# Decoding kept out of the products of sums, and the first two pieces' sums emitted early, in a fused attention and MLP kernel on one core

## The chip, the core and the metric

The kernel runs on one core of one Trainium2 chip. The time is device microseconds of one execution; three executions of the kernel before are given by their median. The engines are TensorE (PE; its weight loads PEld overlap with its matmuls), VectorE (DVE), ScalarE (ACT), GpSimd (POOL) and SyncE (SP), which issues the loads. Each engine takes its instructions in the order in which the program emits them, and an instruction that waits holds up all that stand behind it on its engine.

## The reference

Three stages follow each other. Only the second is touched by the change.

```python
x = banded_attention(q, k, v)              # [2, 768, 512]
h = x.transpose(0, 2, 1) @ U @ V           # mixing along the sequence
u = x + h.transpose(0, 2, 1)
x2 = u + np.maximum(u @ w_ch1, 0) @ w_ch2  # w_ch1 [512, 2048], w_ch2 [2048, 512]
out = gated_mlp(x2, w_in, w_spatial, b_spatial, w_out)
```

The weights come as 64-bit floats and have to be made into 32-bit ones on the chip.

## The kernel before

**Weights.** `Weights` cuts the weights into 28 pieces of 128x1024 elements. Quarter g (0 to 3) of the 2048 hidden columns owns pieces 4g and 4g+1 (columns of `w_ch1`) and 4g+2 and 4g+3 (rows of `w_ch2`). `emit32` decodes a piece in two halves of 128x512: a load by SP into one of three buffers r, a magnitude on ACT (L78, w<-r), and on DVE L83, L84 (w<-w), L90 and L93 (w<-r,w). `emit` then splits a decoded piece w into a high part on ACT (L217, h<-w) and a low part on POOL (L59, l<-w,h), two subtractions of 128x512. There are two buffers for w: piece p can begin only when POOL has read piece p-2 for the last time.

**Sums.** For the first two pieces of quarters 1 to 3 (`quartered`), `quarters` replaces the four blocks of w by differences, in place, with four subtractions on DVE (L234), and splits them as well: th on ACT (L236), tl on POOL (L59). So w comes free only behind tl. For chunks 0 and 1 of 512 tokens, `chunks_by_sums` then makes the products with seven block products instead of eight, fourteen groups of six matmuls for a quarter. The order is X0, X1, Y0, Y1 with h and l, then a pair with S2 (into X), a pair with S1 (into Z), a pair "uh, th" that the text calls S3 (into X), a pair with S4 (into Z) and a last pair. ACT copies (L345, p<-mmm) hold partial results: one of X0 and one of X1 before the S2 pair may write to X, and one of each S2 result before S3 may. A sum is evicted by DVE (L349, s<-mmm,p), ACT (L470, c<-s) and DVE (L471, c<-s,c). The sums S of the activations are made once, in quarter 0, by `sum_rows`: four subtractions on DVE (L325), four copies on ACT (L327) and four subtractions on POOL, twice.

**Order of the work.** A quarter goes: c0, c1 (hidden activations of chunks 0 and 1; by sums in quarters 1 to 3), y0, c2, y1, y2 (outputs of the chunks), where c2 and each y have four groups of twelve matmuls. Groups write to eight PSUM banks in turn, so that a group needs the bank of the group eight before it: y1's that of y0's. DVE frees it, by L471 behind a c group (after L470 on ACT) and L528 (u<-u,mmm) behind a y group. The text writes y1(2) for the group d=2 of y1.

**What emits the decoding.** `run` yields after each group, and `fast` then calls `wt.step(DECODE[1])`, which lets `emit` go on and gives 1.5 us of credit to `emit32`. The rest of the order is plain: what is emitted first stands first on its engine.

Of the kernel before, what the change touches and what calls it, by code (L numbers as in the profile page):

```python
# [52 lines left out]
START, DECODE, MIXING = 20, (0.9, 1.5), (1, 4)  # L53
# [4 lines left out]
def sub(eng, out, a, hi):  # L58
    eng.tensor_tensor(out=out, in0=a, in1=hi.bitcast(F32), op=ALU.subtract)  # L59


def sub_parts(eng, out, a, hi, n):

    m = a.shape[1] // n
    for i in range(n):
        part = slice(i * m, (i + 1) * m)
        sub(eng, out[:, part], a[:, part], hi[:, part])
# [51 lines left out]
class Weights:  # L119
# [88 lines left out]
    def emit(self):  # L208

        nc = self.nc  # L210
        for p, (_, _, a, n) in enumerate(self.order):
            while p >= self.decoded or p - RING >= self.freed:
                yield
            hi = self.ring.tile([P, a, n], F32R, name=f"h{p}", tag="whi")
            lo = self.ring.tile([P, a, n], F32R, name=f"l{p}", tag="wlo")
            wv = self.w32.pop(p)[:, :a * n].rearrange("p (a n) -> p a n", a=a)
            nc.scalar.activation(out=hi, in_=wv, func=AF.Copy)  # L217
            sub_parts(nc.gpsimd, lo, wv, hi, 2)
            if p in self.quartered:
                yield  # L220
                while self.room is None or p - 3 > self.freed:
                    yield
                self.sums[p] = self.quarters(wv)
            self.ready.append((hi, lo))
            yield
# [35 lines left out]
class Moe:  # L261
# [199 lines left out]
    def run(self, u, late):  # L461
# [7 lines left out]
        def evict_c(cp, cc, f):  # L469
            nc.scalar.activation(out=cc[:, 0, f], in_=cp, func=AF.Relu)  # L470
            nc.vector.scalar_tensor_tensor(out=cc[:, 1, f], in0=cp, scalar=0.0, in1=cc[:, 0, f].bitcast(F32),  # L471
                                           op0=ALU.max, op1=ALU.subtract)
# [3 lines left out]
        for g in range(4):  # L476
            w1 = w.take(2)
            w2 = None
            for what, ch in (("c", 0), ("c", 1), ("y", 0), ("c", 2), ("y", 1), ("y", 2)):
                tok = slice(ch * CH, (ch + 1) * CH)  # L480
                if what == "c":
                    cs[ch] = self.q.tile([P, 2, 4, CH], F32R, name="c", tag="Q")
                    if self.room and g and ch < 2:
                        if ch == 1:
                            sums = [w.sums.pop(4 * g + i) for i in range(2)]
                            for _ in self.chunks_by_sums(u, w1, sums, bank, evict_c, cs):
                                yield "g"
                        continue

                    def term(f, ds):  # L490
                        wh, wl = w1[f // 2]
                        fs = slice((f % 2) * P, (f % 2 + 1) * P)
                        return [(wh[:, d, fs], wl[:, d, fs], uh[:, d, tok], ul[:, d, tok]) for d in ds]

                    late_d = g == 0 and ch == 1
                    cps = []
                    if late_d:
                        for f in range(4):
                            cps.append(bank())
                            self.gemm(cps[f], term(f, range(ND - 1)), last=False)  # L500
                            yield "g"
                    for f in range(4):
                        if late_d:
                            cp = cps[f]
                            self.gemm(cp, term(f, [ND - 1]), first=False)
                        else:
                            cp = bank()
                            self.gemm(cp, term(f, range(ND)))
                        evict_c(cp, cs[ch], f)
                        if ch == NCH - 1 and f % 2:  # L510
                            w.free(1)
                        yield "g"
                    if self.room and ch == 1:
                        self.sum_rows(u, 0)
                    continue
                if w2 is None:
                    w2 = w.take(2)
                if g == 3 and ch == 1:
                    x2 = self.pair("x2")
                cc = cs.pop(ch)  # L520
                for d in range(ND):
                    yp = bank()
                    ds = slice(d * P, (d + 1) * P)
                    self.gemm(yp, [(w2[f // 2][0][:, f % 2, ds], w2[f // 2][1][:, f % 2, ds], cc[:, 0, f], cc[:, 1, f])
                                   for f in range(4)])
                    if self.room and g == ch == 0 and d == 1:
                        self.sum_rows(u, 1)
                    nc.vector.tensor_tensor(out=u32[:, d, tok], in0=u32[:, d, tok], in1=yp, op=ALU.add)  # L528
                    if g == 3 and ch:

                        for k in ((), (0, 1), (2,))[ch]:
                            tk = slice(k * CH, (k + 1) * CH)
                            nc.scalar.activation(out=x2[0][:, d, tk], in_=u32[:, d, tk], func=AF.Copy)
                            sub(nc.gpsimd, x2[1][:, d, tk], u32[:, d, tk], x2[0][:, d, tk])
                    if ch == NCH - 1 and d == ND - 1:
                        w.free(2)
                    yield "g"
# [503 lines left out]
def late_pools(tc, ctx, pfx, before=None):  # L1041
    def late():
        if before:
            before.close()
        small = ctx.enter_context(tc.tile_pool(name=pfx + "late", bufs=1))
        return small, small.tile([P, 2, 4, DM], F32R, name="v2")

    return late
# [16 lines left out]
def fast(tc, keep, windows, v, ints, w, out):  # L1065

    nc = tc.nc
    with ExitStack() as ctx:
        cp = ctx.enter_context(tc.tile_pool(name="consts", bufs=1))
        ps = ctx.enter_context(tc.tile_pool(name="ps", bufs=2, space=PSUM))  # L1070
        wt = Weights(tc, ctx, w, "m")
# [37 lines left out]
        fi = keep.tile([P, 1], I32, name="fi")  # L1109

        run, ahead = None, 8
        for i, what in enumerate(a):
            if i >= UVSTART:
                next(uv, None)
            if i > START and i % NT not in MIXING:
                wt.step(DECODE[0])
            if i >= B * PAIRS * NT - 1:
                if run is None:
                    run = moe.run(u, late_pools(tc, ctx, "m", sctx))
                moe.only_scores = what == "tile"  # L1120
                if ahead:
                    next(run)
                    ahead -= 1
# [6 lines left out]
        nc.vector.tensor_tensor(out=flag[:, 3:4], in0=flag[:, 0:1], in1=flag[:, 1:2], op=ALU.max)  # L1130
        nc.vector.tensor_tensor(out=flag[:, 3:4], in0=flag[:, 3:4], in1=flag[:, 2:3], op=ALU.max)
        nc.vector.tensor_copy(fi, flag[:, 3:4])
        for _ in run:
            wt.step(DECODE[1])
    return nl, ng, fi, moe.store_end


# [49 lines left out]
```

## Time and profile before

| | |
|---|---|
| median of three executions | 560.02 us (559.26 to 562.2) |
| the profiled execution | 557.51 us, its span 555.7 us |
[...]
| TensorE busy | 516.5 us (93%) |
| DVE, ACT, POOL busy | 331.3, 226.6, 186.0 us |

The span runs from the first to the last instruction; the 1.8 us that the execution takes beyond it lie around the program. A matmul counts as busy until its modelled end, so that a dense stretch shows TensorE as busy throughout.

### The profile page before, as it was taken

Reading aid. Unit: us, or ns where it says so; the run is one execution under the profiler, and the core shown is the slowest. Engines: PE = TensorE matmul, PEld = TensorE weight load, DVE = VectorE, ACT = ScalarE, POOL = GpSimd, SP = SyncE. Lnnn points to the kernel's source line nnn. Section 1 sums busy time; section 2 is a strip of 40 time slices with the busy share of each in tenths; the row PEclk is TensorE's granted clock in tenths of the full one; section 3 lists DMA queues with packets and bytes.
Section 4 is the critical chain, followed back from the end, with each engine's and each line's share of the span. In section 5 each row is a group of like instructions: output and inputs, shape, how many; then the busy total and the mean of one; then the engine's idle time right before and its main releaser. Section 6 shows DMA issues by size and latency. Waiting matters only on the chain.

```text
span 555.7 us, 7327 instructions
## 1 busy us (share of the span) xinstructions
PE 516.5 (93%) x2744; PEld 433.7 (78%) x2744; DVE 331.3 (60%) x707; ACT 226.6 (41%) x420; POOL 186.0 (33%) x167
## 2 busy tenths in 40 slices
PE   8999998899999589998699994999999999999995
PEld 6888877787887368886488873888888888999884
DVE  6876877556969964299653798726255301594400
ACT  4777887734333331233321334213365423132221
POOL 1233355331665410144200542005874511465000
PEclk9999999999999789999899999899999999999999
DMA  8647453112302420013300143201220110100122
GB/s 292 245 159 248 172 210 136 39 38 79 111 2 75 125 102 0 1 61 130 113 0 1 38 152 112 77 1 38 67 57 1 32 55 0 39 0 2 60 94 80
DMA packets 18237, 45.10 MB, mean 81 GB/s; under 512 B 2448, under 2 KB 5136, under 8 KB 17296
## 3 DMA queue, kind: packets, MB, share of 16 engines
q1 hardware_dynamic: 18048, 44.54, 23.8%
q8 instruction: 23, 0.38, 0.3%
q14 instruction: 22, 0.18, 0.1%
q10 hardware_dynamic: 144, 0.00, 0.0%
HBM read 40.99 MB, written 3.15 MB: 79 GB/s over the span
## 4 chain that ended last, share of the span: by engine, by line
PE 69%; DVE 19%; ACT 5%; issue 3%; POOL 3%; POOLq 0%; DVEq 0%; ACTq 0%
PE mmm L306 18%; PE mmm L307 18%; PE mmm L308 18%; DVE w L93 4%; PE sc L820 4%; DVE w L90 4%; PE pt L844 3%; PE xp L870 3%; DVE u L528 2%; DVE w L83 2%; POOL tl L59 2%; DVE w L84 2%; PE xp L872 2%; DVE w L234 1%; DVE c L471 1%
## 5 line engine op out<-in xcount | busy, mean ns | idle before, releaser
L59 POOL TENSOR_TENSOR l<-w,h 128x512 fp32r<-128x512 f32 (+1 forms) x56 | 76.3, 1386 | 132.8 <-ACT h L217 119.3
L307 PE MATMUL mmm<-c,h 128*128 128x512 f32 x192 | 74.8, 390 | 1.0 <-DVE c L471 1.0
L306 PE MATMUL mmm<-c,h 128*128 128x512 f32 x192 | 74.7, 389 | 0.0
L308 PE MATMUL mmm<-c,l 128*128 128x512 f32 x192 | 74.7, 389 | 0.0
L78 ACT ACTIVATE w<-r 128x512 f32<-128x512 f32 x44 | 28.9, 667 | 54.9 <-POOL l L59 30.0
L834 ACT ACTIVATE e<-s,m 128x256 f32<-128x256 f32 (+1 forms) x96 | 41.7, 482 | 21.0 <-DVE m L831 20.7
L528 DVE TENSOR_TENSOR u<-u,mmm 128x512 f32<-128x512 f32 x48 | 32.5, 682 | 29.6 <-PE mmm L308 29.6
L306 PE MATMUL mmm<-uh,h 128*128 128x512 f32 x120 | 47.5, 396 | 1.2 <-DVE u L528 0.8
L307 PE MATMUL mmm<-ul,h 128*128 128x512 f32 x120 | 46.9, 391 | 0.1
L308 PE MATMUL mmm<-uh,l 128*128 128x512 f32 x120 | 46.8, 390 | 0.0
L471 DVE SCALAR_TENSOR_TENSOR c<-mmm,c 128x512 fp32r<-128x512 f32 x30 | 20.2, 686 | 43.6 <-ACT c L470 43.6
L59 POOL TENSOR_TENSOR tl<-w,th 128x512 fp32r<-128x512 f32 x12 | 16.7, 1413 | 88.1 <-ACT th L236 85.3
L844 PE MATMUL pt<-ident,e 128*128 128x128 f32 x176 | 45.8, 279 | 0.0
L93 DVE SCALAR_TENSOR_TENSOR w<-r,w 128x512 int32<-128x512 int32 x44 | 43.7, 992 | 0.8
L307 PEld LDWEIGHTS mmm<-c,h 128*128 128x128 f32 x192 | 36.0, 188 | 8.8 <-DVE c L471 1.4
L308 PEld LDWEIGHTS mmm<-c,l 128*128 128x128 f32 x192 | 36.0, 188 | 7.5
L306 PEld LDWEIGHTS mmm<-c,h 128*128 128x128 f32 x192 | 36.0, 188 | 7.5
L90 DVE SCALAR_TENSOR_TENSOR w<-r,w 128x512 int32<-128x512 int32 x44 | 40.9, 930 | 0.7
L470 ACT ACTIVATE c<-mmm 128x512 fp32r<-128x512 f32 x30 | 17.1, 590 | 51.8 <-PE mmm L308 51.8
L831 DVE CUSTOM_DVE_ANT_0 s<-sc,bias 128x256 f32<-128x256 f32 (+1 forms) x90 | 32.8, 396 | 7.4 <-ACT e L834 5.9
L217 ACT ACTIVATE h<-w 128x1024 fp32r<-128x1024 f32 (+1 forms) x28 | 28.2, 1007 | 11.4 <-DVE w L93 9.0
L844 PEld LDWEIGHTS pt<-ident,e 128*128 128x128 f32 x176 | 32.3, 190 | 0.7 <-ACT e L834 0.3
(171 smaller groups left out, 1222.1 us busy)
## 6 DMA issues: line engine op xcount, KB each, us to landing
r<-in_w_dram SPq DMA_DIRECT2D x32, 512.0 KB, 3.5
kq<-in_windows_dram SPq DMA_DIRECT2D x7, 1024.0 KB, 6.8
vt<-in_v_dram SPq DMA_DIRECT2D x16, 390.0 KB, 4.2
r<-in_w_in_dram SPq DMA_DIRECT2D x8, 512.0 KB, 3.7
out_dram<-ot SPq DMA_DIRECT2D x11, 256.0 KB, 2.0
w<-in_spT_dram SPq DMA_DIRECT2D x6, 384.0 KB, 3.1
r<-in_w_out_dram SPq DMA_DIRECT2D x4, 512.0 KB, 3.6
kq<-in_windows_dram SPq DMA_DIRECT2D x2, 256.0 KB, 3.7
```

The lines of the kernel that those rows point to most:

```text
L59: eng.tensor_tensor(out=out, in0=a, in1=hi.bitcast(F32), op=ALU.subtract)
L78: nc.scalar.activation(out=mag, in_=raw[..., 1].bitcast(F32), func=AF.Abs)
L90: nc.vector.scalar_tensor_tensor(out=mi, in0=raw[..., 1], scalar=-0x40000000, in1=mi, op0=ALU.bitwise_and, op1=ALU.bitwise_or)
L93: nc.vector.scalar_tensor_tensor(out=oi, in0=raw[..., 0], scalar=29, in1=mi, op0=ALU.logical_shift_right, op1=ALU.bitwise_or)
L217: nc.scalar.activation(out=hi, in_=wv, func=AF.Copy)
L306: self.nc.tensor.matmul(out, lhsT=lh, rhs=rh, start=first and i == 0, stop=False, **kw)
L307: self.nc.tensor.matmul(out, lhsT=lh, rhs=rl, start=False, stop=False, **kw)
L308: self.nc.tensor.matmul(out, lhsT=ll, rhs=rh, start=False, stop=last and i == n - 1, **kw)
L528: nc.vector.tensor_tensor(out=u32[:, d, tok], in0=u32[:, d, tok], in1=yp, op=ALU.add)
L831: nc.vector.tensor_tensor_reduce(out=s[:, :n], in0=sps[hd], in1=bs, scale=-0.125, scalar=3e38, op0=ALU.add, op1=ALU.min, accum_out=m)
L834: nc.scalar.activation(out=e[:, :n], in_=s[:, :n], func=AF.Exp, bias=m, scale=-1.0)
L844: nc.tensor.transpose(pt[:, k * P:(k + 1) * P], es[hd][:, j * P:(j + 1) * P], c["ident"])
```

## The change

Three lines change. A group of products of sums now yields "s", and behind it `step` gets no credit, so that no decoding is emitted there; `emit` still goes on. And the sums of pieces 4 and 5, the first that are quartered, no longer wait until pieces of quarter 0 are freed; those of later quarters wait as before.

```diff
             if p in self.quartered:
                 yield
-                while self.room is None or p - 3 > self.freed:
+                while self.room is None or p - 4 in self.quartered and p - 3 > self.freed:
                     yield
                 self.sums[p] = self.quarters(wv)
...
                             for _ in self.chunks_by_sums(u, w1, sums, bank, evict_c, cs):
-                                yield "g"
+                                yield "s"
...
-        for _ in run:
-            wt.step(DECODE[1])
+        for what in run:
+            wt.step(0.0 if what == "s" else DECODE[1])
```

The first place is in quarter 0, on DVE, from the end of c1 on. Piece 4 is w_1819, piece 5 w_1917, piece 6 w_2113 before and w_1979 now. Before:

```order
L471 SCALAR_TENSOR_TENSOR c<-mmm,c 128x512
L90 SCALAR_TENSOR_TENSOR w_1917<-r_1913,w_1917 128x512
L93 SCALAR_TENSOR_TENSOR w_1917<-r_1913,w_1917 128x512
L325 TENSOR_TENSOR f_1985<-u_79 128x512
...
L528 TENSOR_TENSOR u_79<-u_79,mmm 128x512
L325 TENSOR_TENSOR f_2028<-u_79 128x512
...
L528 TENSOR_TENSOR u_79<-u_79,mmm 128x512 x3
L471 SCALAR_TENSOR_TENSOR c<-mmm,c 128x512 x2
L234 TENSOR_TENSOR w_1819<-w_1819 128x2x128 x4
```

And now, from the L471 of c1(2), one earlier:

```order
L471 SCALAR_TENSOR_TENSOR c<-mmm,c 128x512
L234 TENSOR_TENSOR w_1819<-w_1819 128x2x128 x4
L93 SCALAR_TENSOR_TENSOR w_1917<-r_1864,w_1917 128x512
...
L471 SCALAR_TENSOR_TENSOR c<-mmm,c 128x512
...
L528 TENSOR_TENSOR u_79<-u_79,mmm 128x512
L83 TENSOR_SCALAR w_1979<-w_1979 128x512
L84 TENSOR_SCALAR w_1979<-w_1979 128x512
L90 SCALAR_TENSOR_TENSOR w_1979<-r_1944,w_1979 128x512
L325 TENSOR_TENSOR f_2043<-u_79 128x512
...
L528 TENSOR_TENSOR u_79<-u_79,mmm 128x512
```

The four subtractions of piece 4 moved from behind c2's first two L471 to ahead of c1's last, and three decoding instructions of piece 6 moved in between y0(0)'s L528 and the second four L325, ahead of y0(1)'s L528.

On ACT, at the same place, before:

```order
L217 ACTIVATE h_1951<-w_1819 128x1024
L78 ACTIVATE w_1917<-r_1913 128x512
L470 ACTIVATE c<-mmm 128x512 x2
L327 ACTIVATE uh<-f_1985 128x512
L327 ACTIVATE S1h<-f_1989 128x512
```

And now:

```order
L470 ACTIVATE c<-mmm 128x512
L236 ACTIVATE th<-w_1819 128x1024
L78 ACTIVATE w_1979<-r_1944 128x512
L470 ACTIVATE c<-mmm 128x512
L327 ACTIVATE uh<-f_1996 128x512
```

Piece 4's th and the first magnitude of piece 6 (which needs piece 4's buffer) moved in between the L470 of c1(2) and that of c1(3).

The second place is the start of the products of sums of quarter 2, on DVE. Piece 12 is w_2689, piece 13 w_2783. Before:

```order
L93 SCALAR_TENSOR_TENSOR w_2689<-r_2671,w_2689 128x512
L528 TENSOR_TENSOR u_79<-u_79,mmm 128x512
L83 TENSOR_SCALAR w_2783<-w_2783 128x512
L84 TENSOR_SCALAR w_2783<-w_2783 128x512
L90 SCALAR_TENSOR_TENSOR w_2783<-r_2707,w_2783 128x512
L93 SCALAR_TENSOR_TENSOR w_2783<-r_2707,w_2783 128x512
...
L349 TENSOR_TENSOR s<-mmm,p 128x512
L471 SCALAR_TENSOR_TENSOR c<-s,c 128x512
L90 SCALAR_TENSOR_TENSOR w_2783<-r_2728,w_2783 128x512
L93 SCALAR_TENSOR_TENSOR w_2783<-r_2728,w_2783 128x512
L349 TENSOR_TENSOR s<-mmm,p 128x512
```

And now:

```order
L93 SCALAR_TENSOR_TENSOR w_2689<-r_2671,w_2689 128x512
L528 TENSOR_TENSOR u_79<-u_79,mmm 128x512
L349 TENSOR_TENSOR s<-mmm,p 128x512
L471 SCALAR_TENSOR_TENSOR c<-s,c 128x512
L349 TENSOR_TENSOR s<-mmm,p 128x512
```

All eight decoding instructions of piece 13 moved out; they stand behind the products now, between the L528 of y0.

On ACT, at the same place, before (piece 12's high part is h_2796, piece 11 is w_2627):

```order
L217 ACTIVATE h_2778<-w_2627 128x1024
L78 ACTIVATE w_2783<-r_2707 128x512
L345 ACTIVATE p<-mmm 128x512
L217 ACTIVATE h_2796<-w_2689 128x1024
L78 ACTIVATE w_2783<-r_2728 128x512
L345 ACTIVATE p<-mmm 128x512
L470 ACTIVATE c<-s 128x512 x2
```

And now:

```order
L217 ACTIVATE h_2778<-w_2627 128x1024
L78 ACTIVATE w_2783<-r_2707 128x512
L345 ACTIVATE p<-mmm 128x512
L217 ACTIVATE h_2796<-w_2689 128x1024
L345 ACTIVATE p<-mmm 128x512
L470 ACTIVATE c<-s 128x512 x2
```

The second magnitude of piece 13 moved to y0; the first one still stands ahead of the first p. Quarters 1 and 3 read alike at this place, with pieces 9 and 17 for 13 (in quarter 3 both halves of piece 18 leave too).

## Rows read from the trace of the kernel before

**Rows 1.** Waits of TensorE by releaser: us in total, times, longest us.

```profile
PE mmm L306 <- ACT p L345: 22.4, 9, 4.9
```

**Rows 2.** Stretches: length, busy us (x instructions) by engine, clock, DMA share, GB/s.

```profile
203.46:211.75 8.29, 8.29 (x36) 6.86 (x37) 4.61 (x8) 3.30 (x6) 0.00 (x0) 1.00 0.09 38
...
211.75:233.51 21.76, 21.76 (x97) 18.02 (x96) 7.77 (x14) 3.86 (x6) 0.91 (x1) 1.00 0.00 1
273.81:278.26 4.45, 4.45 (x12) 3.50 (x13) 1.20 (x3) 2.04 (x4) 0.00 (x0) 0.62 0.20 79
346.56:355.02 8.46, 8.46 (x24) 6.67 (x25) 6.82 (x12) 2.75 (x6) 0.00 (x0) 0.64 0.46 150
```

**Rows 3.** Timeline of TensorE: start, length, instruction [idle before, releaser].

```profile
203.46 0.50 PE L306 MATMUL mmm<-uh,th 128*128 128x512 f32 x1 [2.17 <-ACT p L345]
...
261.70 0.50 PE L306 MATMUL mmm<-S2h,th 128*128 128x512 f32 x1 [0.83 <-ACT p L345]
...
265.31 0.51 PE L306 MATMUL mmm<-S2h,th 128*128 128x512 f32 x1 [1.95 <-ACT p L345]
...
273.81 0.50 PE L306 MATMUL mmm<-uh,th 128*128 128x512 f32 x1 [4.12 <-ACT p L345]
...
337.27 0.50 PE L306 MATMUL mmm<-S2h,th 128*128 128x512 f32 x1 [1.51 <-ACT p L345]
...
346.56 0.80 PE L306 MATMUL mmm<-uh,th 128*128 128x512 f32 x1 [4.92 <-ACT p L345]
```

**Rows 4.** Timeline of DVE, ACT and POOL, start of quarter 2's products of sums.

```profile
263.05 0.68 DVE L528 TENSOR_TENSOR u<-u,mmm 128x512 f32<-128x512 f32 x1
...
264.13 0.66 ACT L78 ACTIVATE w<-r 128x512 f32<-128x512 f32 x1
264.35 2.99 POOL L59 TENSOR_TENSOR l<-w,h 128x512 fp32r<-128x512 f32 x2 [3.89 <-issue]
...
264.68 0.58 ACT L345 ACTIVATE p<-mmm 128x512 f32<-128x512 f32 x1
...
266.23 1.66 DVE L93 SCALAR_TENSOR_TENSOR w<-r,w 128x512 int32<-128x512 int32 x1
...
268.61 0.68 DVE L349 TENSOR_TENSOR s<-mmm,p 128x512 f32<-128x512 f32 x1
...
269.99 0.69 DVE L471 SCALAR_TENSOR_TENSOR c<-s,c 128x512 fp32r<-128x512 f32 x1 [0.70 <-ACT c L470]
...
271.93 0.68 DVE L349 TENSOR_TENSOR s<-mmm,p 128x512 f32<-128x512 f32 x1
```

**Rows 5.** The same at quarter 3.

```profile
335.00 0.68 DVE L528 TENSOR_TENSOR u<-u,mmm 128x512 f32<-128x512 f32 x1
...
336.31 2.99 POOL L59 TENSOR_TENSOR l<-w,h 128x512 fp32r<-128x512 f32 x2 [3.43 <-issue]
```

**Rows 6.** Timeline of quarter 0, from the end of c1 to the first products of sums.

```profile
138.99 3.08 POOL L59 TENSOR_TENSOR l<-w,h 128x512 fp32r<-128x512 f32 x2 [9.59 <-ACT h L217]
...
145.26 1.29 DVE L325 TENSOR_TENSOR f<-u 128x512 f32<-128x512 f32 x2
...
148.90 0.68 DVE L528 TENSOR_TENSOR u<-u,mmm 128x512 f32<-128x512 f32 x1
...
156.67 0.39 PE L306 MATMUL mmm<-c,h 128*128 128x512 f32 x1
...
158.70 2.41 DVE L234 TENSOR_TENSOR w<-w 128x256 f32<-128x256 f32 x4
...
166.03 0.69 DVE L471 SCALAR_TENSOR_TENSOR c<-mmm,c 128x512 fp32r<-128x512 f32 x1 [4.93 <-ACT c L470]
...
170.96 0.50 PE L307 MATMUL mmm<-c,h 128*128 128x512 f32 x1 [0.98 <-DVE c L471]
...
177.70 0.43 DVE L83 TENSOR_SCALAR w<-w 128x512 f32<-128x512 f32 x1 [0.21 <-ACT w L78]
...
192.70 0.68 DVE L528 TENSOR_TENSOR u<-u,mmm 128x512 f32<-128x512 f32 x1
```

## The prediction, made before the changed kernel was run

> **What bounds the kernel now.** I read the page first, then the waits of TensorE, its timeline at each of them, and the timelines of the engines that release them. TensorE is busy for 93% of the span, so only its idle time and its slow stretches can be won. Nearly all of its idle time has one releaser, the copy p on ACT: nine waits, 22.4 us [rows 1]. They come three to a quarter with products of sums: before the two S2 groups and before S3. A dense group of twelve matmuls takes 2.72 us at full clock (21.76 us for 96, so 0.227 us for one) [rows 2]. [...]
>
> Why p is late shows in quarter 2 [rows 4]. The last L528 of y2 is at 263.05; then DVE decodes piece 13 for 5 us, because POOL splits piece 12 at the same time (264.35, 2.99 us) and L93 takes 1.66 us beside it, against 0.69 for an L471 of the same form with POOL idle. Only at 268.61 comes the first L349, at 271.93 the second, with L90 and L93 of the second half between them. On ACT, the p of the S2 results stands behind both c<-s copies, which wait for the two L349. S3 starts at 273.81 [rows 3].
>
> **The change, term by term.** I work out when S3 starts in each of the three quarters, since from there to the next decoding TensorE ran without a wait, and that work is not changed.
>
> *Quarter 2.* DVE: the eight decoding instructions are gone, so the first L349 follows the L528, at 263.05 + 0.60 = 263.65. ACT: the second p no longer stands behind a magnitude (264.13 to 264.68, 0.55 us), so the second S2 group starts at 265.31 - 0.55 = 264.76. Before, TensorE was ready for S3 at 273.81 - 4.12 = 269.69, 4.38 us behind the start of that group; now at 269.14. Is p in time for that? From L349 to its L471 there were 1.38 us (269.99 - 268.61). ACT reaches c<-s only behind the second p, 0.3 us later than it might. The L471 then falls beside POOL's splitting. No row shows an L471 with both inputs in SBUF beside POOL: its bounds are 0.69, and 1.66 like L93, which is nearest, with two inputs in SBUF too; I take 1.66. From the second L349 to S3 there were 1.88 us (273.81 - 271.93). Sum: 263.65 + 0.3 + 1.38 + 1.66 + 1.88 = 268.9 at most, 0.2 us before TensorE is ready. So S3 starts at 269.14, 4.67 us earlier, and without the long wait before it the twelve matmuls take 2.72 and not 4.45 us: another 1.73. **6.4 us.** Bounds: 4.4 if p is 2 us late after all (a wait of that length did not cost the clock); 8.6 if the two S2 waits, 0.83 and what is left of 1.95, 1.40 [rows 3], shrink to nothing too. They should not: the first p still stands behind the first magnitude of piece 13.
>
> *Quarter 3.* The same: the second S2 group at 337.27 - 0.55 = 336.72, TensorE ready for S3 4.37 us behind it (346.56 - 4.92 - 337.27), at 341.09. The first L349 comes at 335.60 [rows 5], its c<-s behind the second p at about 336.64; 0.66 + 1.66 + 1.88 behind that is 340.84, in time. S3 starts 5.47 us earlier, and 24 matmuls take 5.44 and not 8.46 us: 3.02. **8.5 us**; by the same bounds 6.5 to 10.3 (0.96 left of 1.51, and 0.83 as in quarter 2).
>
> *Quarter 1, and the early sums in quarter 0* [rows 6]. Here the change also adds waits. L234 of piece 4 overwrites what POOL's l4 reads, so it begins at 138.99 + 3.08 = 142.1. Behind it ACT makes th, POOL tl, ACT the first magnitude of piece 6 (in the buffer that tl frees), and only then the L470 of c1(3), on whose L471 DVE waits with everything behind it. This round trip is in the trace, one chunk later: 158.70 to 166.03, 7.33 us, 4.93 of them with DVE idle. So that L471 is at 149.4, 6 us later than before. L90 and L93 of piece 5 (1.3) and its own 0.6 bring the first L325 to 151.3, and y0(0)'s L528 to 3.64 us later (148.90 - 145.26), 154.95: in time for y1(0) at 156.67, which needs its bank. Then come three instructions of piece 6, beside the four subtractions of S on POOL: between 1.6 us (alone) and 5.0 (three at 1.66); I take 4, nearer the second. The second four L325 start at 159.6 and y0(1)'s L528 ends at 163.9. y1(1) wants that bank at 156.67 + 2.72 = 159.4: a new wait of about 4.5 us. Piece 6's remaining five instructions, two L528 and three L471 end at 171.4; the sums of piece 5 go through a second round trip, and the L471 of c2(3) starts at 178.7 and ends at 179.4, where TensorE stood waiting for it at 170.96 before: 8.4 us later, a second new wait of 4 us or so.
>
> From there decoding is ahead. Before, DVE went from the first L83 of piece 7 (177.70) to the last L528 (192.70) in 15.0 us; with one more L528 (0.6) and the last one itself (0.6) the first L349 is at 179.4 + 16.2 = 195.6, and S3 1.38 + 1.66 + 1.88 later, at 200.5, against 203.46. TensorE alone, at full clock, would be there at 179.4 + 0.45 + 8.16 + 5.44 + 5.44 = 198.9; through its S2 waits (h7 must wait for the end of y2, then l7 and a magnitude stand before the first p) it comes to about the same 200.4. So 3.0 us; from which I take 1.5 for the clock, which the two new waits of 4 us may take as the old ones did (1.73 and 3.02 us there; the first is hidden behind DVE's lateness, the second only partly). **1.5 us.** Bounds: a gain of 4.6 if POOL slows nothing; a loss of 5 if all eight L90 and L93 of pieces 7 and 8 take 1.66 (two do now; 6 us) and the clock costs 1.7 more.
>
> [...]
>
> *What is moved behind the products* must fit there. In y0 and c2 of quarter 1 DVE was busy for 7.77 of 21.76 us [rows 2], 14 us free; the eight instructions take 4.5 us there with POOL idle (four at 0.43 like the L83 of [rows 6], four at 0.69), 6.2 at the price that they had (268.61 - 263.65 and 271.93 - 269.99 - 0.69). The sums of piece 8 and all behind them then start when they did, relative to TensorE. In quarter 3 it is twice as much, with no sums behind it. SP's loads keep their order; each is issued when an L93 frees its buffer and is needed only from c2 on, so their moving costs nothing as long as DVE keeps up. POOL gets nothing more; tl4 stands before the eight subtractions of S instead of behind, which is in the round trip. If the cover in y0 were gone, the next quarter's first p would be later by up to those 6.2 us.
>
> **Sum.** 1.5 + 6.4 + 8.5 = 16.4 us. The span of 555.7 becomes 539.3, the execution's 557.51 becomes 541.1; the median shown is 2.5 us above that execution, so I predict 560.02 - 16.4 = 543.6 us.
>
> **Rivals.** *Quarter 1 gives back more*: its two new waits at the bounds above, S3 at 208 instead of 202. For it: the long hold behind L78, and POOL beside DVE. Against it: DVE has less to do before S3 than before. 543.6 + 7 = 551. *S3 still waits*, because my margin of 0.2 us in quarters 2 and 3 is not there: 2.5 us left in each and the clock falling as before, 2.5 + 1.7 + 2.5 + 3.0 = 9.7 more, 553. For it: the slowed L471; against it: with the L471 at 0.69 there is a margin of 1.2. *The S2 waits shrink too*, to nothing: 0.83 and 1.40 in quarter 2, 0.83 and 0.96 in quarter 3, 539.6. For it: less on ACT; against it: the first p's place has not changed. *Slower*: the moved decoding does not fit into y0 and c2, and what was taken out of one quarter's products comes back as a later first p in the next. It decides from the point at which DVE's free 14 us are used up, then every us is paid in TensorE idle: quarters 2 and 3 would win nothing (+14.9), quarter 1 would lose its 5 instead of winning 1.5 (+6.5), together 565. Against it: 14 free and 6.2 asked.
>
> **How the numbers follow.** My forecast 0.65, quarter 1 giving back 0.15, S3 still waiting 0.08, the S2 waits gone 0.07, slower 0.05. The likeliest case by itself lies between 540 and 550. With the two cases above and the one below, the range is 538 to 552; what is left out is the slower case and the ends of two others. 0.5% (2.8 us) is about what a measurement of this kernel can tell from no change: faster 0.91, same 0.04, slower 0.05.
>
> **What would show it.** In the profile of the changed kernel: no wait before S3 of over 1 us in quarters 2 and 3 and a clock of 1.00 behind it; S2 waits like those of before, the second half a microsecond shorter; in quarter 0 two new waits of TensorE of 4 to 5 us, one released by L528 in y1, one by L471 at the start of y2; DVE idle for some 4 us behind L234 of piece 4 and again of piece 5; more DVE work, but no new wait, in y0. I am wrong if S3 still waits, if quarter 1's S3 starts behind 206, or if a wait shows in the y0 or c2 of quarters 1 to 3.

## The result and the profile after

The changed kernel takes 540.94 us (median of four, 540.29 to 541.74); the kernel before took 560.19 in the same measurement (four, 559.26 to 562.2). The ratio is 0.965, 95% interval 0.962 to 0.968. The profiled executions are 540.54 and 557.51 us, their spans 538.7 and 555.7: 17.0 us apart. TensorE is busy for 95% of the span.

The waits of TensorE (us in all, times, longest), where [rows 1] had 22.4 us in nine for p:

```profile
PE mmm L306 <- ACT p L345: 4.4, 4, 1.4
PE mmm L306 <- DVE u L528: 4.1, 2, 3.8
...
PE mmm L306 <- ACT c L470: 3.3, 1, 3.3
```

Four short waits for p are left. The wait for L470 is new, and that for L528 has grown: in the kernel before it was one wait of 0.81 us, in quarter 1. Where they stand, in TensorE's timeline (as [rows 3]):

```profile
162.87 0.50 PE L306 MATMUL mmm<-c,h 128*128 128x512 f32 x1 [3.75 <-DVE u L528]
...
179.21 0.50 PE L306 MATMUL mmm<-c,h 128*128 128x512 f32 x1 [3.35 <-ACT c L470]
...
259.36 0.50 PE L306 MATMUL mmm<-S2h,th 128*128 128x512 f32 x1 [0.83 <-ACT p L345]
...
262.42 0.51 PE L306 MATMUL mmm<-S2h,th 128*128 128x512 f32 x1 [1.40 <-ACT p L345]
...
266.62 0.39 PE L306 MATMUL mmm<-uh,th 128*128 128x512 f32 x1
...
331.98 0.39 PE L306 MATMUL mmm<-uh,th 128*128 128x512 f32 x1
```

The long waits before S3 (4.12 and 4.92 us) are gone, S3 at 266.62 and 331.98 waits for nothing. The new waits are those of y1(1) and of y2(0). Stretches by engine (columns as in [rows 2]):

```profile
162.87:170.43 7.56, 7.55 (x24) 5.44 (x24) 7.49 (x7) 2.42 (x5) 6.73 (x5) 0.77 0.23 72
179.93:190.28 10.35, 10.35 (x39) 8.38 (x40) 10.14 (x16) 3.03 (x5) 2.92 (x3) 0.84 0.32 100
...
209.41:231.17 21.76, 21.76 (x98) 18.02 (x96) 11.88 (x22) 4.42 (x7) 0.91 (x1) 1.00 0.15 49
266.62:271.07 4.45, 4.45 (x21) 3.71 (x20) 1.98 (x3) 1.34 (x3) 0.00 (x0) 1.00 0.00 0
331.98:340.14 8.16, 8.16 (x37) 6.76 (x36) 4.43 (x7) 2.50 (x4) 0.00 (x0) 1.00 0.00 0
```

From S3 on the granted clock (in the profile a share of TensorE's full speed) is 1.00 in quarters 2 and 3, where it was 0.62 and 0.64. In y0 and c2 of quarter 1 DVE works 11.88 us instead of 7.77, for eight more instructions, and TensorE still fills all of the 21.76 us. The first two rows are the stretches behind the new waits: at a clock of 0.77 on average 24 matmuls take 7.56 us, and at 0.84 the 38 matmuls that start in the second row (it counts one more that ends there) 10.35 us, where full clock makes them 5.44 and 8.6 (0.227 each). DVE was busy for 7.49 of the 7.56 us.

DVE, ACT and POOL at the start of quarter 2's products of sums (as [rows 4]):

```profile
260.71 0.68 DVE L528 TENSOR_TENSOR u<-u,mmm 128x512 f32<-128x512 f32 x1
260.82 1.06 ACT L217 ACTIVATE h<-w 128x1024 fp32r<-128x1024 f32 x1 [1.52 <-DVE w L93]
261.31 0.68 DVE L349 TENSOR_TENSOR s<-mmm,p 128x512 f32<-128x512 f32 x1
...
262.01 2.99 POOL L59 TENSOR_TENSOR l<-w,h 128x512 fp32r<-128x512 f32 x2 [3.90 <-issue]
...
262.92 0.93 DVE L471 SCALAR_TENSOR_TENSOR c<-s,c 128x512 fp32r<-128x512 f32 x1 [0.93 <-ACT c L470]
...
263.77 0.68 DVE L349 TENSOR_TENSOR s<-mmm,p 128x512 f32<-128x512 f32 x1
...
265.02 1.56 ACT L345 ACTIVATE p<-mmm 128x512 f32<-128x512 f32 x3
```

L349 follows the L528 at once, 0.60 us behind its start (5.56 before), and the L471 that I priced at 1.66 beside POOL takes 0.93. The first of the three p is done at about 265.6, a microsecond before S3. And quarter 0 (as [rows 6]):

```profile
147.22 0.66 ACT L78 ACTIVATE w<-r 128x512 f32<-128x512 f32 x1 [2.70 <-POOL tl L59]
...
148.39 0.69 DVE L471 SCALAR_TENSOR_TENSOR c<-mmm,c 128x512 fp32r<-128x512 f32 x1 [3.62 <-ACT c L470]
...
154.57 0.92 DVE L83 TENSOR_SCALAR w<-w 128x512 f32<-128x512 f32 x1
...
155.16 1.47 POOL L59 TENSOR_TENSOR S2l<-f,S2h 128x512 fp32r<-128x512 f32 x1
155.53 1.40 DVE L84 TENSOR_SCALAR w<-w 128x512 int32<-128x512 int32 x1
156.60 1.47 POOL L59 TENSOR_TENSOR S4l<-f,S4h 128x512 fp32r<-128x512 f32 x1
156.96 1.66 DVE L90 SCALAR_TENSOR_TENSOR w<-r,w 128x512 int32<-128x512 int32 x1
...
162.14 0.68 DVE L528 TENSOR_TENSOR u<-u,mmm 128x512 f32<-128x512 f32 x1
...
179.18 0.69 DVE L471 SCALAR_TENSOR_TENSOR c<-mmm,c 128x512 fp32r<-128x512 f32 x1 [4.86 <-ACT c L470]
```

The two round trips show as DVE's idle 3.62 and 4.86 us ahead of an L471 whose L470 stands behind a magnitude, which waits for tl. Between them, three decoding instructions beside POOL's subtractions, 3.98 us together; then the L528 for which y1(1) waits.

### The profile page after: what moved, and what is told of

It is laid out like the page before. It is cut to its first block, busy times and chain, and to the rows that moved or that the text cites. A ratio compares the mean times of both kernels' runs of the same rounds, so it can differ in the third digit from the quotient of the medians.

```text
span 538.7 us, 7333 instructions
## 1 busy us (share of the span) xinstructions
PE 510.5 (95%) x2744; PEld 430.2 (80%) x2744; DVE 325.1 (60%) x707; ACT 226.5 (42%) x420; POOL 183.8 (34%) x167
## 4 chain that ended last, share of the span: by engine, by line
PE 52%; DVE 9%; ACT 2%; issue 2%; POOL 1%; POOLq 0%; DVEq 0%
PE mmm L307 17%; PE mmm L306 17%; PE mmm L308 17%; DVE w L90 2%; DVE w L93 2%; DVE w L234 1%; DVE u L528 1%; POOL tl L59 1%; DVE w L84 1%; DVE w L83 1%; DVE c L471 1%; ACT th L236 1%; ACT w L78 1%; ACT c L470 0%; ACT h L217 0%
## 5 line engine op out<-in xcount | busy, mean ns | idle before, releaser
L59 POOL TENSOR_TENSOR l<-w,h 128x512 fp32r<-128x512 f32 (+1 forms) x56 | 74.8, 1358 | 125.2 <-ACT h L217 106.9
L306 PE MATMUL mmm<-c,h 128*128 128x512 f32 x192 | 76.3, 398 | 7.5 <-DVE u L528 4.1
L307 PE MATMUL mmm<-c,h 128*128 128x512 f32 x192 | 76.2, 397 | 0.2 <-DVE c L471 0.2
L308 PE MATMUL mmm<-c,l 128*128 128x512 f32 x192 | 76.0, 396 | 0.0
L306 PEld LDWEIGHTS mmm<-c,h 128*128 128x128 f32 x192 | 36.7, 191 | 16.8 <-DVE u L528 5.4
L471 DVE SCALAR_TENSOR_TENSOR c<-mmm,c 128x512 fp32r<-128x512 f32 x30 | 20.2, 686 | 43.8 <-ACT c L470 43.8
L307 PEld LDWEIGHTS mmm<-c,h 128*128 128x128 f32 x192 | 36.8, 191 | 8.2 <-DVE c L471 0.5
L528 DVE TENSOR_TENSOR u<-u,mmm 128x512 f32<-128x512 f32 x48 | 32.5, 682 | 14.4 <-PE mmm L308 14.4
L90 DVE SCALAR_TENSOR_TENSOR w<-r,w 128x512 int32<-128x512 int32 x44 | 39.0, 887 | 0.7
L93 DVE SCALAR_TENSOR_TENSOR w<-r,w 128x512 int32<-128x512 int32 x44 | 38.8, 881 | 0.7
L470 ACT ACTIVATE c<-mmm 128x512 fp32r<-128x512 f32 x30 | 17.2, 591 | 39.0 <-PE mmm L308 39.0
L603 DVE TENSOR_TENSOR gs<-mmm,bsp 128x384 f32<-128x384 f32 x16 | 8.8, 550 | 40.6 <-PE mmm L308 40.6
```

Source lines behind the costliest of these rows:

```text
L90: nc.vector.scalar_tensor_tensor(out=mi, in0=raw[..., 1], scalar=-0x40000000, in1=mi, op0=ALU.bitwise_and, op1=ALU.bitwise_or)
L93: nc.vector.scalar_tensor_tensor(out=oi, in0=raw[..., 0], scalar=29, in1=mi, op0=ALU.logical_shift_right, op1=ALU.bitwise_or)
L306: self.nc.tensor.matmul(out, lhsT=lh, rhs=rh, start=first and i == 0, stop=False, **kw)
L307: self.nc.tensor.matmul(out, lhsT=lh, rhs=rl, start=False, stop=False, **kw)
L308: self.nc.tensor.matmul(out, lhsT=ll, rhs=rh, start=False, stop=last and i == n - 1, **kw)
```

## The experiments

To compare runs I take, from each trace, where S3 starts. The first column counts from the matmul on which all have waited for the last uh, at the end of attention (131.72 us into the span before, 131.28 after; 130.8 to 131.9 in all others but one), the next two from one S3 to the next. All are differences of starts in TensorE's timeline.

```
                          to S3     S3 of 1   S3 of 2   S3 of 3   span
                          of q. 1   to of 2   to of 3   to end
before                    71.74     70.35     72.75     209.14    555.7
changed                   69.88     65.46     65.36     206.72    538.7
e1  late sums             67.31     65.37     65.38     206.74    536.5
e2  early sums only       75.37     72.51     72.83     209.47    561.0
e4  no credit at c1(2)    69.81     65.47     65.49     206.76    539.2
e7  some decoding back    72.47     68.17     66.54     207.01    545.5
e9  first p free          68.59     66.99     65.39     206.30    540.9
e8  e1 + hold of three    62.87     62.70     62.56     205.88    525.6
e10 e1 + hold of four     61.36     62.56     62.56     206.39    524.8
e11 e1 + hold of six      58.86     71.08     71.33     213.36    546.0
e12 changed + hold        70.54     62.56     62.56     206.32    533.7
changed, repeat           70.55     65.37     65.49     206.28    539.2
before, repeat            71.72     70.33     72.81     208.62    555.1
```

The kernel before took 557.5 to 558 us in these measurements (medians). e1, e2, e4 and e7 shared a chip, as did e8, e9 and the two repeats, and e10 to e12.

**e1: decoding kept out, sums late.** Against the changed kernel:

```diff
-                while self.room is None or p - 4 in self.quartered and p - 3 > self.freed:
+                while self.room is None or p - 3 > self.freed:
```

> Only one half of the change: the decoding is kept out of the products of sums, but the sums of pieces 4 and 5 wait as in the kernel before, so that quarter 0 runs as before up to the first product of sums. My theory: the whole gain comes from the decoding kept out, and the early sums take some of it back in quarter 1, since they make TensorE wait twice (3.75 and 3.35 us in the profile of the changed kernel). In the profile: no wait in y1 and y2 of quarter 0 but the 0.98 us of before, y2 starts at 170.96, S3 of quarter 1 starts at 199 to 201 (201.16 in the changed kernel, 203.46 before), quarters 2 and 3 as in the changed kernel. Time about 540.0 (538.5 to 541.5). The rival, that the early sums are what helps quarter 1: S3 of quarter 1 at 203 or later, 542.8 or more.

Measured: 538.24 us, ratio 0.965 (0.962 to 0.968). TensorE's timeline in quarter 1:

```profile
191.31 0.79 PE L306 MATMUL mmm<-S2h,th 128*128 128x512 f32 x1 [4.92 <-ACT p L345]
...
199.01 0.39 PE L306 MATMUL mmm<-uh,th 128*128 128x512 f32 x1
```

Although its first S2 wait of 4.92 us stays, S3 of quarter 1 comes 2.6 us earlier than in the changed kernel; the other quarters are the same to 0.1 us. So the early sums cost something, and this half alone is the whole gain and 2.2 us of span more. Its time lies a little under my range.

**e2: sums early, decoding in the products.** Against the kernel before:

```diff
-                while self.room is None or p - 3 > self.freed:
+                while self.room is None or p - 4 in self.quartered and p - 3 > self.freed:
```

> Only the other half: the sums of pieces 4 and 5 early, and the decoding in the products of sums as before. My theory: the two new waits of TensorE in quarter 0 delay everything on DVE by 5 to 8 us, and with piece 9 decoded ahead of the first L349 nothing makes up for it: the first L349 of quarter 1 at about 201 to 203, its S3 at 206 to 208 (203.46 before), a wait of 4 us or more before it and the clock down behind it; quarters 2 and 3 with the waits of before (4.12 and 4.92 us). Time 564 (561 to 567), so slower than before. The rival, that early sums help by themselves, because less stands before the products: 559 or less.

Measured: 562.74 us, ratio 1.009 (1.005 to 1.012), slower by not quite 1%. TensorE's timeline:

```profile
206.19 0.80 PE L306 MATMUL mmm<-uh,th 128*128 128x512 f32 x1 [5.04 <-ACT p L345]
```

As expected: a wait of 5.04 us in place of 2.17, and 2.2 us more from this S3 to the next (72.51 instead of 70.35), with the granted clock at 0.71 over the 7.8 us behind the wait. The parts don't add up: -19.2 and +5.3 us of span make -13.9, both together -17.0. With early sums quarter 1 has no S2 wait of 4.92 us, since TensorE gets there late; that this is the difference is argued, not shown.

**e4: no credit behind c1(2).** `HOLD` is `(2,)`, the number of that group, counted from c1(0). One more line shifts this kernel's numbers by one.

```diff
-        for what in run:
+        for n, what in enumerate(run):
...
-            wt.step(0.0 if what == "s" else DECODE[1])
+            wt.step(0.0 if what == "s" or n in HOLD else DECODE[1])
```

> The changed kernel, with one credit less: behind the group c1(2) of quarter 0 none is given, so that the first magnitude of piece 6, which waits for the low part of the sums of piece 4, is emitted behind the L470 of c1(3) and no longer ahead of it. My theory: that magnitude is what makes the first of the two round trips (3.6 us of idle DVE before the L471 at 148.39), so this wait goes, y1(1) no longer waits 3.75 us for its bank, what follows on DVE comes about 3 us earlier, and S3 of quarter 1 starts at 198 to 199.5 instead of 201.16. Time 538.2 (537 to 539.5). The rival, that DVE is too full there in any case, because the subtractions of the sums and the decoding beside POOL are what delays it: the wait moves to another instruction, S3 stays at about 201, 541.

Measured: 541.08 us, ratio 0.970 (0.966 to 0.973). TensorE's timeline:

```profile
161.18 0.50 PE L307 MATMUL mmm<-c,h 128*128 128x512 f32 x1 [1.67 <-DVE u L529]
...
165.73 0.50 PE L307 MATMUL mmm<-c,h 128*128 128x512 f32 x1 [1.54 <-DVE u L529]
...
169.31 0.50 PE L307 MATMUL mmm<-c,h 128*128 128x512 f32 x1 [0.55 <-DVE u L529]
...
179.04 0.80 PE L307 MATMUL mmm<-c,h 128*128 128x512 f32 x1 [4.67 <-ACT c L471]
```

My theory fell. The first round trip is gone (the L471 of c1(3), here L472, starts at 145.42 and no longer at 148.39), but the wait in y1 is only split: 1.67 + 1.54 + 0.55 = 3.76 us, as much as the 3.75. DVE is full there (busy for 15.69 of the 16 us from 154 to 170), and the second round trip then sets y2 as before. The rival was right: S3 of quarter 1 stays where it was (69.81 and 69.88).

**e7: one credit back behind the first group of products.**

```diff
+        last = None
...
-            wt.step(0.0 if what == "s" else DECODE[1])
+            wt.step(0.0 if what == last == "s" else DECODE[1])
+            last = what
```

> The changed kernel, with part of the decoding put back: one credit behind the first group of each quarter's products of sums, so that three decoding instructions (L83, L84, L90 of pieces 9, 13, 17) stand ahead of the first L349 again, and a magnitude ahead of the second p, but none between the two L349. My theory: the chain from the last L528 over the first L349 to S3 is what TensorE waits for, the changed kernel has only about 1 us to spare there, and three instructions of 2.8 us beside POOL use that up and 1.5 to 2 us more: a wait before S3 of 1.5 to 2.5 us in every quarter with products of sums, too short to cost much clock. Time 547 (545 to 549). The rival, that only the second half's L90 and L93 between the two L349 made TensorE wait: no wait before S3, 541.

Measured: 547.47 us, ratio 0.981 (0.978 to 0.984). TensorE's timeline, then a stretch:

```profile
203.78 0.50 PE L306 MATMUL mmm<-uh,th 128*128 128x512 f32 x1 [2.19 <-ACT p L345]
...
271.95 0.50 PE L306 MATMUL mmm<-uh,th 128*128 128x512 f32 x1 [0.31 <-ACT p L345]
```

```profile
203.78:208.24 4.46, 4.46 (x13) 3.50 (x14) 1.58 (x3) 2.04 (x4) 0.00 (x0) 0.62 0.00 0
```

The sum came out, its parts did not. Quarter 1 lost 2.6 us and 1.7 more to the clock (24 matmuls from S3 on take 7.19 us at a granted clock of 0.76, not 5.53). Quarters 2 and 3 lost 1.1 and 1.2: 0.57 before the second S2 group (1.97 us instead of 1.40, the magnitude ahead of p) and 0.3 before S3. The margin of about 1 us that I had counted on is there (in the changed kernel p is ready at 265.6, S3 starts at 266.62); what I left out is what covers the delay besides it. In quarter 2 the three instructions put the first L349 2.5 us behind its place, but p follows it in 3.8 us instead of 4.3, and TensorE itself comes 0.6 us later.

**e8, e10, e11: less decoding ahead of the products.** e1 with no credit behind the last three groups of y2, behind all four, and behind six groups (two of y1 as well), in quarters 0 to 2. Below is the list of e8; that of e10 begins at 16, 46 and 76, that of e11 at 14, 44 and 74.

```diff
-        for what in run:
-
+        for n, what in enumerate(run):
+            what = "s" if n in (17, 18, 19, 47, 48, 49, 77, 78, 79) else what
             wt.step(0.0 if what == "s" else DECODE[1])
```

> The kernel with late sums and no decoding in the products of sums, and in quarters 0 to 2 no credit behind the last three groups of y2 either: the second half of pieces 8, 12 and 16 and the first magnitude of pieces 9, 13 and 17 move to the next y0, so that neither p of X0 and X1 stands behind a magnitude or an h, and the first L349 stands right behind the last L528. My theory: the waits that are left before the S2 groups (4.92 us in quarter 1, 0.82 and 1.40 in quarter 2, 1.27 and 0.94 in quarter 3 of the kernel with late sums) come from this decoding alone and go with it, and y0 and c2 have room for four more instructions: S3 of quarter 1 about 6 us earlier (192 to 193.5 instead of 199.0, the clock included), quarters 2 and 3 about 2.2 us each. Time 528 (526 to 531). The rival, that y0 and c2 or the start of the last stage have no room for more: the S2 waits go, but new waits come behind c2's L471 or behind y2 of quarter 3, 534 or more.

Measured: 528.35 us, ratio 0.947 (0.944 to 0.950). S3 of quarter 1 comes 4.4 us earlier than in e1, not 6, and quarters 2 and 3, without any S2 wait, win 2.7 and 2.8, not 2.2. What is left in quarter 1, in the timelines of TensorE and DVE:

```profile
187.05 0.50 PE L306 MATMUL mmm<-S2h,th 128*128 128x512 f32 x1 [0.75 <-ACT p L345]
...
190.59 0.68 DVE L349 TENSOR_TENSOR s<-mmm,p 128x512 f32<-128x512 f32 x1
...
194.46 0.50 PE L306 MATMUL mmm<-uh,th 128*128 128x512 f32 x1 [1.68 <-ACT p L345]
```

> Late sums, no decoding in the products of sums, and no credit behind all four groups of y2 in quarters 0 to 2 (one more than in the run with three): two more instructions of piece 8 (12, 16), L90 and L93 of the first half, move to y0. My theory: what is left in quarter 1, a wait of 1.68 us before S3 behind a first L349 at 190.59, comes from this decoding ahead of the last L528 (one L93 there takes 1.66 us beside POOL), and goes; y0 of quarter 1 has 2.2 us of DVE free in 10.9 and c2 4.4, so two instructions of 1.4 us alone and 3.3 us beside POOL fit. Quarters 2 and 3 have no wait left to win. Time 526.7 (525.5 to 528), 1.7 below the run with three. The rival, that the decoding is now late enough to be missed: the sums or the low parts of the next pieces come late, a new wait of 1 us or more in c2 or y1 and 529 or more.

Measured: 526.38 us, ratio 0.944 (0.940 to 0.947): the fastest version, by 0.8 us of span against e8 (the intervals of the two ratios overlap). S3 of quarter 1 is 1.5 us earlier and doesn't wait, though one S2 wait of 1.10 us is left there, and from S3 to S3 it takes 62.56 us, the length without any wait.

> The same with no credit behind the last two groups of y1 and all of y2: eight more instructions than in the run with three stand in y0 and c2 (in the later quarters too), 4.5 us of DVE alone and 6.2 beside POOL. My theory: this is beyond the point from which moved decoding comes back; DVE has 6.6 us free in y0 and c2 of the run with three, so that it ends close to where c2 does, and the sums, whose round trip over ACT and POOL stands there, push L471 of c2: new waits of TensorE of 2 to 4 us in y1 or y2 of quarters 1 and 2, with the clock behind them. Time 533 (529 to 540). The rival, that there is still room, since decoding that is emitted later is only decoded later: 526.7 as with four.

Measured: 548.35 us, ratio 0.983 (0.980 to 0.987), outside my range. DVE, ACT and TensorE at the start of y0 in quarter 1:

```profile
202.68 0.69 DVE L93 SCALAR_TENSOR_TENSOR w<-r,w 128x512 int32<-128x512 int32 x1
203.41 1.06 ACT L217 ACTIVATE h<-w 128x1024 fp32r<-128x1024 f32 x1 [2.13 <-DVE w L93]
204.51 0.75 PE L306 MATMUL mmm<-c,h 128*128 128x512 f32 x1 [4.60 <-ACT h L217]
...
206.08 0.80 PE L308 MATMUL mmm<-c,l 128*128 128x512 f32 x1 [0.39 <-POOL l L59]
```

There is a point from which it is slower, but not where I put it. Products of sums come even earlier (58.86), and then y0 itself stands still, because its weights, piece 7 (11, 15), are not decoded: 4.60 us in each of three quarters, 0.3 to 0.8 for l, and the clock (0.54 over the 7.49 us from 204.51 on); 8.5 and 8.8 us more from one S3 to the next than in e10. What ends the room is the first user of the piece, not DVE's free time.

**e9: the first magnitude of pieces 9, 13 and 17 behind the products.** On top of e1:

```diff
-                magnitude(p + j, 1 - j)
+                p + j in (9, 13, 17) and j or magnitude(p + j, 1 - j)
```

(and no credit behind the last group of y2, so that it does not follow there.)

> The kernel with late sums and no decoding in the products of sums, and in it the first magnitude of pieces 9, 13 and 17 is emitted with the second one, behind the products, so that the first p stands behind h of piece 7 (11, 15) alone; DVE's order ahead of the products is unchanged. My theory: what sets the S2 pair is not this magnitude but the decoding of piece 8 (12, 16) on DVE, for whose end the h ahead of the second p waits. So the wait before the first S2 group shrinks (4.92 us in quarter 1 to 1 or 2, 0.82 and 1.27 to less), the one before the second grows by as much, and S3 stays where it is: 538 (536.5 to 539.5). The rival, that the magnitude in front of the first p is what TensorE waits for: the S2 waits go for good, 5 us less in quarter 1 and about 1 in each of the others, 532.

Measured: 541.77 us, ratio 0.970 (0.967 to 0.974). TensorE's timeline, then two stretches:

```profile
189.31 0.50 PE L306 MATMUL mmm<-S2h,th 128*128 128x512 f32 x1 [0.96 <-ACT p L345]
...
196.37 0.80 PE L306 MATMUL mmm<-S2h,th 128*128 128x512 f32 x1 [5.40 <-ACT p L345]
...
263.38 0.50 PE L306 MATMUL mmm<-S2h,th 128*128 128x512 f32 x1 [2.52 <-ACT p L345]
...
330.39 0.50 PE L306 MATMUL mmm<-S2h,th 128*128 128x512 f32 x1 [2.52 <-ACT p L345]
```

```profile
263.38:269.21 5.83, 5.83 (x19) 4.63 (x19) 2.22 (x3) 2.66 (x5) 2.56 (x2) 0.71 0.16 61
...
330.39:334.60 4.21, 4.21 (x19) 3.48 (x19) 2.22 (x3) 2.56 (x5) 2.58 (x2) 1.00 0.33 111
```

The rival is out: with the magnitude gone from in front of the first p, the first wait shrinks from 4.92 to 0.96 us and the second becomes 5.40. What I missed is the clock, and with it the time: waits made one cost 1.3 us in quarter 1 (a granted clock of 0.70 over the 5.85 us from 196.37 on) and 1.6 in quarter 2 (0.71). In this profile attention is also 2 us longer (133.63 to the starting matmul), for which I have no reason.

**e12: the changed kernel with e8's hold.**

> The changed kernel, early sums and all, with no credit behind the last three groups of y2 of quarters 0 to 2. My theory: quarters 2 and 3 win what they win with late sums (2.7 and 2.8 us), and quarter 1 nothing, because there TensorE is late from y2 of quarter 0 on and waits for no p: its S3 stays 70 us behind the start of the sequence's last mixing, where the run with late sums and the same hold has it at 63. The early sums, which cost 2.2 us in the changed kernel, cost 7 here. Time 534.5 (533 to 536.5). The rival, that the early sums' cost stays 2.2 us whatever stands in quarter 1: 530.5.

Measured: 536.1 us, ratio 0.961 (0.957 to 0.964). The waits of y1(1) and y2(0) are 3.71 and 3.35 us. S3 of quarter 1 in TensorE's timeline:

```profile
202.26 0.39 PE L306 MATMUL mmm<-uh,th 128*128 128x512 f32 x1
```

Quarter 1 gains nothing, the others everything. But the hold did less in quarter 1 than in e8: DVE's order up to the first L349 is the changed kernel's, instruction by instruction, with one half of a piece more decoded ahead of it than in e8; only the first magnitude of piece 9 moved, on ACT. S3 waits for nothing there, TensorE is busy without a gap from the end of y2 on and gets to S3 when it does in the repeat of the changed kernel (70.54 and 70.55). So TensorE's own lateness sets S3, as I had it; what the early sums would cost with as little decoding ahead as e8 has is not measured. The 7.7 us between e8 and e12 before S3 of quarter 1, against 2.6 between e1 and the changed kernel, contain that difference too.

**Repeats.** Nothing was changed in either.

> The changed kernel once more, unaltered, beside the others on one chip. 540.5 (539 to 542); if the early sums cost what the traces say, it is 2 to 2.5 us above the kernel with late sums, 538.2, and the same as the one without a credit behind c1(2), 541.1.

Measured: 540.43 us, ratio 0.968 (0.965 to 0.972), as expected. Its S3 of quarter 1 is 0.7 us later than in the first profile (70.55 instead of 69.88 in the table), though both new waits are as long (3.75 and 3.35 us): y2 from its wait on takes 11.74 us (179.44 to 191.18) instead of 11.07 (179.21 to 190.28).

```profile
202.06 0.39 PE L306 MATMUL mmm<-uh,th 128*128 128x512 f32 x1
```

> The kernel before once more, unaltered, for a second profile: the profiled execution was 2.7 us faster than its median, that of the changed kernel at its median. If this comes from TensorE's clock behind the long waits, the two profiles differ in the stretches behind waits of 2 to 5 us, by 1 to 2 us in each, and are alike elsewhere. If it comes from DMA or from attention, they differ ahead of the first products of sums. Time 558 to 560.

Measured: 558.5 us (twelve executions, 556.79 to 560.53), ratio 1.000; the profiled one 556.94. Its waits stand where [rows 3] has them, within 0.2 us, but for S3 of quarter 1, a stretch of which follows:

```profile
203.34 0.50 PE L306 MATMUL mmm<-uh,th 128*128 128x512 f32 x1 [2.43 <-ACT p L345]
```

```profile
203.34:206.06 2.72, 2.72 (x12) 2.27 (x13) 0.87 (x2) 1.64 (x4) 0.00 (x0) 1.00 0.34 133
```

Both profiles of the kernel before are of executions below its median, so they can't tell why others take up to 5 us more. At the same mean clock, 0.98, the spans of this run go from 555.0 to 558.6.

## Why the prediction was right, step by step

**Quarter 2.** Predicted 6.4 us, measured 6.6: 70.35 - 65.46 = 4.9 to S3, and 1.7 behind it, where twelve matmuls take 2.72 us again. The steps hold: L349 right behind L528, the second p without a magnitude, TensorE and not p setting S3. One price was wrong. The L471 beside POOL takes 0.93 (0.92 in quarter 3, 1.22 in quarter 1) and not 1.66, so that the margin is 1.0 us and not 0.2. The rows of quarter 0 suggest why no fixed price fits: L84 and L90, alone 0.43 and 0.69 us, both end 0.13 to 0.14 us before the end of POOL's instruction plus their own time (L84: 155.16 + 1.47 + 0.43 = 157.06, against 156.93; L90: 158.76 against 158.62). My reading, which no run tests, is that each got on only when POOL's instruction was over, so that its delay depends on when in that instruction it comes. The L471 of quarter 2 fits: POOL's first subtraction ends at 263.30, and 0.69 behind that is 263.99, against 263.85.

**Quarter 3.** Predicted 8.5 us, measured 8.7 (S3 to y0 took 11.18 us before, 8.16 now, and S3 is 17.6 - 3.0 - 8.9 = 5.7 us further ahead).

**Quarter 1.** Predicted 1.5, measured 1.9 to S3 in the first profile and 1.2 in the repeat. Both new waits are there, at y1(1) and y2(0), with 3.75 and 3.35 us for my 4.5 and 4, and DVE idles for 3.62 and 4.86 us behind the L234; the L471 are at 148.39 and 179.18 where I had 149.4 and 178.7, the three decoding instructions between take 3.98 where I took 4. Two errors then meet. DVE, ACT and TensorE at S3:

```profile
196.70 0.68 DVE L349 TENSOR_TENSOR s<-mmm,p 128x512 f32<-128x512 f32 x1
...
200.47 2.04 ACT L345 ACTIVATE p<-mmm 128x512 f32<-128x512 f32 x4
...
201.16 0.46 PE L306 MATMUL mmm<-uh,th 128*128 128x512 f32 x1
```

The first L349 is at 196.70, not 195.6; and most of the 1.5 us for the clock were not due in this sum. The clock did fall (to 0.77 and 0.84 on average over the two stretches, with 2.1 us lost behind the first wait and 1.7 behind the second), but the first loss ended in another wait for DVE, and little of the second is left at S3: the first p before S3 is done at 201.05, S3 starts at 201.16. In the repeat, where the second loss was 0.7 us larger, p is done at 201.64 and S3 starts at 202.06. So the clock cost 0.1 and 0.4 us at S3; that without it S3 would come from p alone is argued from these rows, not shown. That an L349 over 1 us too early and a charge over 1 us too high nearly cancel is luck.

On TensorE itself both new waits cost clock, 2.1 and 1.7 us, where the two old ones cost 1.73 and 3.02. Charging those 4.75 us in full, instead of the 1.5, would have put the time 3.2 us higher, because it takes every such loss for a loss at the end. It is one only where TensorE is the last to arrive: in e4 the first charge is missing (the clock stays at 1.00 behind the waits of 1.67, 1.54 and 0.55 us) and TensorE only waits longer at y2 for it (4.67 us, not 3.35); in e9 and in the repeat TensorE is last, and S3 is later by what the clock took more.

**What is moved behind the products** took 4.1 us more of DVE in y0 and c2 (4.5 was my figure with POOL idle) and no wait, as said. There is a slower case, as e11 shows, but by another mechanism than my rival's: I put its limit at DVE's 14 free us, and it is the piece that y0 itself reads.

**The S2 waits.** In quarters 2 and 3 they stayed, as predicted, but my reason was wrong. (In quarter 3 the first of them is 1.27 us before and 1.28 now; the 0.83 that I took over from quarter 2 made my upper bound there 0.4 us too low.) In quarter 1 they are gone, where I still had them: TensorE gets there at 195.72, and p is done at 193.98. For quarter 2 I had them behind the first magnitude of piece 13. e9 takes that away, and the wait moves to the second S2 group; e8 takes the decoding of piece 12 from DVE, and it goes. The second p stands behind h of piece 12, which waits for that decoding.

**Sum.** 0.4 ahead of the products, 1.9 + 6.6 + 8.7, less 0.6 that the end gives back (6.8 us behind the last matmul, 6.2 before) make the 17.0 of span, for a predicted 16.4. For a profiled execution the sum gave 541.1, and it was 540.54. What made 543.6 too high by 2.7 us is mostly the step behind the sum: I carried the 2.5 us by which the median before lay above its profiled execution over to the changed kernel, whose median lies only 0.4 above its own. By the medians of the later measurements of the kernel before, 557.5 to 558, the same sum would have given 541.1 to 541.6. The nine executions of the changed kernel and its repeat lie within 2.6 us, the four, seventeen and twelve of the kernel before within 2.9, 5.9 and 3.7; whether what was removed makes that difference is not shown.

Of the change, the decoding kept out is worth 19.2 us of span alone, and the early sums take 2.2 of these back (no execution of e1 took more than 539.88 us, none of the changed kernel less than 539.99).

## What to carry to other kernels

Work that is due later should not stand in front of a chain that TensorE waits for, on any of the engines of that chain; taking it out of the chain gave 19.2 us of span (e1), and 11.7 more lay just ahead of the chain (e10 against e1). A wait that is freed at one place is only gone if nothing behind it on the same engine needs the same thing (e9: 4.92 us became 0.96 and, one group on, 5.40) and the engine is not full there (e4: 3.75 us became 3.76 in three). How far work can be moved back is set by who reads it first: against e8, two instructions more were a gain of 0.8 us of span (e10), eight a loss of 20 (e11).

## What the runs showed of the hardware

In these runs TensorE's clock did not follow from the length of a single wait. Behind the waits of 3.35 us and more in this stage it fell each time (25 waits in all profiles together; over the 7 us behind each the granted clock was 0.50 to 0.76 on average). Behind those of 1.2 to 1.97 us it stayed at 1.00 each time, and behind 2.17 and 2.43 us it stayed at 1.00 too (both profiles of the kernel before, S3 of quarter 1); behind 2.19 at the same place it fell, to 0.62 on average over 4.46 us (e7). Behind two waits of 2.52 us it was 0.71 in quarter 2 and 1.00 in quarter 3 (e9), though TensorE had been busy throughout the 10.9 us ahead of both, at 1.00. So waits of 2 to 2.5 us can go either way here, and why is open.

In quarter 0 of the changed kernel L84, with one input, took 1.40 us beside POOL instead of 0.43, and L90, with two, 1.66 instead of 0.69: 0.97 us more for each.
